# Routing edges to their nodes in two passes: chunks of 24 tiles, fixed rows for each digit, rows stored at their own fronts

## The chip, the core and the metric

The kernel runs on one core of a Trainium2 chip. The time is the device time of one launch in microseconds, the median of several runs; three runs of the kernel before took 8648.92, 8650.12 and 8655.76 us. A profile is one further execution with the hardware profiler on.

## What is computed

A message-passing layer on a graph of 10,000 nodes and 640,000 edges with random ends, 64 channels of 4 components:

```python
R = _silu(edge_feat @ w_rad)                              # (E, C)
xs = x[src]                                                 # (E, C, M)
tp = jnp.einsum('eci,ef,ifo->eco', xs, Y, cg)             # (E, C, M)
msg = R[:, :, None] * tp
agg = _segment_sum(msg.reshape(-1, C * M), dst, N).reshape(N, C, M)
return jnp.einsum('ncm,cd->ndm', agg, w_mix)
```

## The kernel before

The edges come in no order, and each must meet the sum of its node `dst`. So they are sorted by `dst` first, in two passes, as words of W = 9 floats: a key (14 bits of `src`, `dst` above them, a tag), the four of Y and the four of edge_feat. A tile is 128 edges, one a partition; there are 5000.

Pass 1 (`pass1`) sends each edge to one of 18 groups of 576 nodes in DRAM (`grp`), pass 2 (`pass2`) each word of a group to one of its 18 buckets of 32 nodes (`bkt`), 313 buckets in all. A bucket has room for BT = 17 tiles. All of it is done in three parts (`SPLIT`, 30, 35.5 and 34.5% of the edges), which take 5, 6 and 6 of the 17 tiles of a bucket: while one part is consumed, the next is sorted.

Both passes move words with the same two functions:

- `tables` counts, for the chunks of a batch, how many words of each digit (group or bucket) every tile has, and makes from the counts the place where each chunk's words of a digit begin (`sb`) and the row in DRAM where each of its 128 rows goes (`idx`). It is a chain of small operations on PE, ACT and DVE through one PSUM bank that all callers share.
- `route` takes chunk after chunk (12 tiles in pass 1, 11 in pass 2). `places`, `placed` and `slots` give each word a row and a slot within the row; rows have 14 or 15 slots and belong to one digit each. `spread` (line 519) multiplies a mask of slots (line 524) with the tile's words, so that each word stands in its slot of X and zeros elsewhere (line 527), and makes the one-hot of rows `oh`, six tiles on ACT (lines 542 and 543), the others on DVE (line 536). `move` multiplies the two on PE, tile by tile, into one PSUM bank (line 550); in pass 2 one more matmul (line 552) takes over the row that the chunk before left partly filled. `evict` copies to `rt` (line 557), and `store` writes 128 rows of 504 or 540 bytes with one indirect DMA from POOL (line 561). The stores of a pass are declared free of order among themselves.

A digit that has no room left sends rows to an overflow region.

`messages` then handles the buckets, in 939 units of 5 or 6 tiles. `gather` (line 817) fetches the 1024-byte rows of x by `src`, one indirect DMA a tile, five units ahead into seven buffers. `turn`, `turned`, `radial` and `silu` make R (lines 830 to 843), `spots` makes S, the one-hot of the node times Y (lines 851 and 854), `products` multiplies the gathered rows by R (line 861), and `sums` adds their outer products into G, 24 matmuls a unit (line 872). `evict` adds the sum of earlier parts, fetched by SP (lines 886 and 901), and `mix` applies the weights for four buckets.

Order: in the first stage part 0 goes through pass 1 alone, while the regions in DRAM are cleared. In `groups` the units of `messages` run in quarter steps, and steps of pass 2 for the next group and of pass 1 for the next part are put between them by the numbers that the generators yield (`HEAVY`) and that `pass2_steps` sums. PE, DVE and ACT issue in the order written there. The last group, which is smaller than the others (40 tiles, 9 buckets in part 0), comes first. At the end `overflow` (line 1031) takes what overflowed, 128 slots a round, through a loop that gathers, multiplies, reads the output rows, adds and writes them.

Of the kernel before, what the change touches and what calls it, by code (L numbers as in the profile page):

```python
# [18 lines left out]
F = mybir.dt.float32  # L19
# [6 lines left out]
P = 128  # L26
B = 18
W = 9
# [4 lines left out]
GN = B * NB  # L33
# [5 lines left out]
HEAVY = 4  # L39
BIG = 16384.0  # L40
FAR = 2097152.0


class Pass:


    def __init__(self, T, r, cap, act, carry):
        self.T, self.r, self.cap, self.act, self.carry = T, r, cap, act, carry
        self.stride = 1 << (cap + P - 1).bit_length()
        self.rw = r * W  # L50

        assert T * P + B * (2 * r - 2 if carry else r - 1) < (P + 1) * r and cap >= P
# [19 lines left out]
class Kernel:  # L72
    def __init__(self, ctx, tc, x, src, dst, Y, ef, w_rad, cg, w_mix, out):
# [8 lines left out]
        self.ef = ef.rearrange("(p t) f -> p t f", p=P)  # L82
        self.w_rad, self.cg, self.w_mix = w_rad, cg, w_mix
# [6 lines left out]
        N, E, T, r = self.N, self.E, 12, 14  # L90
        assert N <= 1 << 14 and BT == sum(sum(u) for _, u in SPLIT)
        self.NG = (N + GN - 1) // GN
        assert self.NG <= B
# [5 lines left out]
        self.gt = []  # L99
        for a, z in self.part:  # L100
            nch = (z - a + T - 1) // T
            e = [min(GN, N - g * GN) * (z - a) * P / N for g in range(self.NG)]
            self.gt.append([math.ceil((m + (r - 1) / 2 * nch + 4.5 * math.sqrt(m + (r * r - 1) / 12 * nch)) / P)
                            for m in e])
        NG = self.NG
        self.p1 = Pass(T, r, max(map(max, self.gt)) * P // r, 6, False)
        self.p2 = Pass(11, 15, BT * P // 15, 6, True)

        self.gbase = [[(k * NG + g) * self.p1.stride + self.p1.cap - self.gt[k][g] * P // r for g in range(NG)]
                      for k in range(len(SPLIT))]  # L110
        self.NBK = (N + NB - 1) // NB
# [5 lines left out]
        self.p1.ovf = len(SPLIT) * NG * self.p1.stride  # L117
        self.p2.ovf = self.NBK * self.p2.stride
        for q, tiles in ((self.p1, [z - a for a, z in self.part]), (self.p2, sum(self.gt, []))):
            q.none = -(-(q.ovf + sum((t + q.T - 1) // q.T for t in tiles) * P + 16) // q.stride) * q.stride  # L120
            q.rows = q.none
        self.p1.key, self.p2.key = "grp", "bkt"
        self.xw = max(q.T * q.rw for q in (self.p1, self.p2))
        assert max(q.T + q.carry for q in (self.p1, self.p2)) <= 12

        self.p1.NC, self.p2.NC = 24, max(-(-t // self.p2.T) for t in sum(self.gt, []))
        self.p1.dst = self.dr.tile([self.p1.rows, self.p1.rw], F, name="grp")
        self.p2.dst = self.dr.tile([self.p2.rows, self.p2.rw], F, name="bkt")

        self.sums = self.dr.tile([self.NBK, P, 256], F, name="sums")  # L130
        self.in_group = {"grp": 0, "bkt": 0}
# [10 lines left out]
    def consts(self):  # L142
# [8 lines left out]
        self.zr = c.tile([16, max(self.p1.rw, self.p2.rw)], F, name="zr")  # L151
# [8 lines left out]
        self.iB, self.i32 = self.dv[:, 0:B], self.dv[:, 0:NB]  # L160
# [8 lines left out]
        self.U2 = c.tile([32, 2, 32], F, name="U2")  # L169
        self.id2 = c.tile([64, 32], BF, name="id2")  # L170
        for h in range(2):
            nc.vector.tensor_copy(self.U2[:, h, :], self.U[:32, :32])
            nc.vector.tensor_copy(self.id2[32 * h:32 * h + 32, :], self.ident[:32, :32])
        for p in (self.p1, self.p2):

            p.on = c.tile([64, B * (p.T + 1)], F, name="on" + p.key)
            nc.vector.memset(p.on, 1.0)
            nc.vector.memset(p.on.rearrange("p (b t) -> p b t", b=B)[:, :, 0:1], 0.0)
            p.cols = c.tile([64, B * (p.T + 1)], F, name="cols" + p.key)
            nc.vector.memset(p.cols, 0.0)  # L180
        self.Ub = c.tile([P, P], BF, name="Ub")
        nc.vector.tensor_copy(self.Ub, self.U)
        self.A = c.tile([P, P], BF, name="A")
        nc.vector.scalar_tensor_tensor(self.A, self.ident, BIG, self.U, op0=OP.mult, op1=OP.add)
# [8 lines left out]

        self.gb, self.gc = [], []
        for k in range(len(SPLIT)):
            gb = iota("gb%d" % k, [[self.p1.stride, B]], base=k * self.NG * self.p1.stride)
            gc = c.tile([P, B], F, name="gc%d" % k)
            nc.vector.memset(gc, 0.0)
            for g in range(self.NG):
                nc.vector.memset(gb[:, g:g + 1], float(self.gbase[k][g]))  # L200
                nc.vector.memset(gc[:, g:g + 1], float(self.gt[k][g] * P // self.p1.r))
            self.gb.append(gb)
            self.gc.append(gc)

        self.k1 = c.tile([1, B], F, name="k1")
        self.k2 = c.tile([1, self.NG * B], F, name="k2")
# [3 lines left out]
        self.bb = iota("bb", [[self.p2.stride, B]])  # L210
        self.bn = iota("bn", [[NB, B]])
        self.bc = c.tile([P, B], F, name="bc")
        nc.vector.memset(self.bc, float(self.p2.cap))

    def clear_groups(self, k, eng):

        q = 2048
        for g in range(self.NG):
            n = self.gt[k][g] * W
            v = self.group_words(k, g)  # L220
            for o in range(0, n, q):
                m = min(q, n - o)
                eng.dma_start(v[:, o:o + m], self.z[:, :m])
                yield

    def group_words(self, k, g):

        o = self.gbase[k][g] * self.p1.rw
        v = self.p1.dst.rearrange("r w -> (r w)")[o:o + self.gt[k][g] * P * W]
        return v.rearrange("(p q) -> p q", p=P)  # L230

    def bucket_words(self, b, n, t0, t1):

        v = self.p2.dst[:self.p2.ovf, :].rearrange("(b s) w -> b (s w)", s=self.p2.stride)
        return v[b:b + n, t0 * P * W:t1 * P * W].rearrange("b (p q) -> p b q", p=P)

    def clear_buckets(self):
        nc, n = self.nc, 2048 // (BT * W)
        for b in range(0, self.NBK, n):
            m = min(n, self.NBK - b)  # L240
            nc.sync.dma_start(self.bucket_words(b, m, 0, BT),
                              self.z[:, :m * BT * W].rearrange("p (b q) -> p b q", b=m))
            yield
# [44 lines left out]
    def digits(self, D, dig, nt):  # L288

        for o in range(0, nt, 24):  # L290
            m = min(24, nt - o)
            self.onehot(D[:, o:o + m, :], dig[:, o:o + m], m)
            yield

    def onehot(self, D, dig, m):
        self.nc.vector.tensor_tensor(D, self.iB.unsqueeze(1).to_broadcast([P, m, B]),
                                     dig.unsqueeze(2).to_broadcast([P, m, B]), op=OP.is_equal)

    def floor(self, out, x, r, up, nm, n):

        nc = self.nc
        t = self.ph.tile([P, B], I32, name="ri", tag="ri" + nm, bufs=1)
# [3 lines left out]
    def tables(self, ps, D, nt, rows, kov, base, cap):  # L306
# [28 lines left out]
        if not ps.carry:  # L335
            self.floor(R[:H], n[:H], r, True, ps.key, H)
# [844 lines left out]
```

## Time and profile before

| | |
|---|---|
| median of the timed runs | 8650.12 us (8648.92 to 8655.76) |
| span of the profiled execution | 10572.8 us |
| mean granted clock of TensorE | 0.846 |
| indirect DMAs of POOL: gathers, stores | 5321, 958 |
| matmul instructions | 51381 |
| moved by DMA | 1057.31 MB, mean 100 GB/s |

The profiled execution is the slower one by 22%. Of its own time only the span is known. A float32 matmul is two instructions in the trace, each with a weight load (PEld) that can overlap it. In the groups of instructions, a row holds the line, engine, operation, out<-in with their shapes, the count, the busy time and the mean ns of one, and the idle time of the engine before them with what ended it.

### The profile page before, as it was taken

The page shows a single profiled execution, that of the slowest core. Times are in us where ns is not written, and L with a number is a line of the kernel's source. Part 1 is how long each engine was busy: PE and PEld are TensorE (multiplying, and loading weights), DVE is VectorE, ACT ScalarE, POOL GpSimd, SP SyncE. Part 2 cuts the span into 40 slices and gives each one's busy share as a digit, 9 for nine tenths or more (in the row PEclk, how much of TensorE's full clock was granted, in tenths as well). Part 3 has the DMA queues.
Part 4 walks back from the last instruction along what each step waited for, and adds up shares of the span by engine and source line. Part 5 has one row for each costly group of instructions (what it writes and reads, how often), then busy time and mean ns, then how long its engine had stood idle before and what let it go on. Part 6 is the DMA issues. An engine that isn't in the chain of part 4 may idle for free. (4 is left out here: it accounts for less than half of the span.)

```text
span 10572.8 us, 147096 instructions
## 1 busy us (share of the span) xinstructions
PE 8237.0 (78%) x51381; PEld 6957.0 (66%) x51381; DVE 6980.3 (66%) x12762; ACT 3997.5 (38%) x11789; POOL 6029.5 (57%) x6306
## 2 busy tenths in 40 slices
PE   6867877888788777787787787777777887878775
PEld 5756766667677666666676666656666666666664
DVE  6876767777776676776676776656565655656543
ACT  5754444444444343443343333322232222323220
POOL 1225655556565555566566655666666666666664
PEclk8978888888888888888888888878888888888887
DMA  8213333333333333333333333333333333333332
GB/s 165 78 40 90 96 93 90 94 95 97 94 98 92 95 92 103 105 108 111 102 105 110 109 104 104 103 110 112 104 99 104 104 100 106 100 106 99 104 106 74
DMA packets 696316, 1057.31 MB, mean 100 GB/s; under 512 B 251979, under 2 KB 500327, under 8 KB 695576
## 3 DMA queue, kind: packets, MB, share of 16 engines
q0 software_dynamic: 286560, 746.72, 24.8%
q1 hardware_dynamic: 406424, 293.41, 10.2%
q8 instruction: 406, 6.65, 0.3%
q10 hardware_dynamic: 2592, 7.78, 0.2%
q14 instruction: 334, 2.74, 0.1%
HBM read 856.49 MB, written 207.52 MB: 101 GB/s over the span
## 5 line engine op out<-in xcount | busy, mean ns | idle before, releaser
L817 POOL DMA_INDIRECT xg<-in_x_dram,sidx x5321 | 5057.6, 950 | 2989.6 <-issue 1374.4
L872 PE MATMUL G<-S,xg 128*128 128x128 f32 x21284 | 3223.2, 314 | 803.8 <-issue 408.1
L872 PEld LDWEIGHTS G<-S,xg 128*128 128x128 f32 x21284 | 3060.0, 228 | 924.5 <-issue 488.9
L550 PE MATMUL pr<-X,oh 128*128 128x126 f32 (+1 forms) x21286 | 3093.3, 302 | 696.8 <-issue 404.7
L550 PEld LDWEIGHTS pr<-X,oh 128*128 128x128 f32 x21286 | 2880.2, 212 | 928.4 <-issue 576.3
L861 DVE TENSOR_TENSOR xg<-xg,pre 128x1536 f32<-128x1536 f32 (+1 forms) x939 | 1557.4, 1659 | 587.0 <-ACT pre L843 440.0
L527 DVE TENSOR_TENSOR X<-dv,Wt 128x1485 f32<-128x1485 f32 (+5 forms) x958 | 1600.4, 1671 | 426.7 <-remote 182.3
L542 ACT ACTIVATE sq<-i,rowf 128x128 f32<-128x128 f32 x5658 | 1751.8, 394 | 9.9 <-DVE rowf L514 6.9
L843 ACT ACTIVATE pre<-pre 128x384 f32<-128x384 f32 (+1 forms) x939 | 429.1, 457 | 3098.6 <-remote 1406.6
L543 ACT ACTIVATE oh<-sq,ones 128x896 f32<-128x896 f32 (+2 forms) x958 | 937.3, 978 | 206.3 <-remote 57.9
L840 PE MATMUL pre<-wr,sT 54*128 54x384 f32 (+1 forms) x1878 | 902.0, 562 | 134.7 <-ACT sT L835 71.4
L854 DVE TENSOR_TENSOR S<-dv,pay 128x768 f32<-128x768 f32 (+1 forms) x939 | 857.3, 913 | 181.6 <-remote 86.2
L561 POOL DMA_INDIRECT bkt<-rt,idx x541 | 542.1, 1002 | 670.5 <-ACT rt L557 405.7
L561 POOL DMA_INDIRECT grp<-rt,idx x417 | 415.2, 996 | 791.7 <-ACT rt L557 388.2
L536 DVE TENSOR_TENSOR oh<-dv,rowf 128x640 f32<-128x640 f32 (+3 forms) x922 | 800.1, 868 | 0.4 <-remote 0.4
L901 DVE TENSOR_TENSOR Gs<-old,G 128x256 f32<-128x256 f32 x313 | 131.2, 419 | 1006.9 <-remote 552.4
L840 PEld LDWEIGHTS pre<-wr,sT 54*128 54x128 f32 (+1 forms) x1878 | 302.0, 200 | 386.5 <-issue 220.6
L901 DVE TENSOR_TENSOR Gp<-old,G 128x256 f32<-128x256 f32 x313 | 130.6, 417 | 538.1 <-remote 310.7
L557 ACT ACTIVATE rt<-pr 128x135 f32<-128x135 f32 (+1 forms) x958 | 257.3, 269 | 519.7 <-remote 230.9
L830 PEld LDWEIGHTS pre<-ident,pay 128*54 128x54 f32 (+1 forms) x939 | 109.0, 116 | 494.1 <-issue 310.3
L835 ACT ACTIVATE sT<-pre 54x128 f32<-54x128 f32 (+1 forms) x939 | 244.3, 260 | 429.5 <-remote 232.2
L830 PE MATMUL pre<-ident,pay 128*54 128x128 f32 (+1 forms) x939 | 294.1, 313 | 87.9 <-DVE xg L861 54.3
(214 smaller groups left out, 5296.4 us busy)
## 6 DMA issues: line engine op xcount, KB each, us to landing
xg<-in_x_dram,sidx POOLq DMA_INDIRECT x5321
sums<-Gp SPq DMA_DIRECT2D x626, 128.0 KB
old<-sums SPq DMA_DIRECT2D x626, 128.0 KB
bkt<-z SPq DMA_DIRECT2D x24, 994.5 KB
pay<-bkt SPq DMA_DIRECT2D x34, 486.0 KB
ys<-in_Y_dram SPq DMA_DIRECT2D x104, 96.0 KB
es<-in_edge_feat_dram SPq DMA_DIRECT2D x104, 96.0 KB
out_dram<-ot SPq DMA_DIRECT2D x69, 128.0 KB
```

The lines of the kernel that those rows point to most:

```text
L527: nc.vector.tensor_tensor(X[:, :m, :].rearrange("p t (s w) -> p t s w", w=W), msk.unsqueeze(3).to_broadcast([P, m, ps.r, W]), QD[c // Q][1 ...
L536: nc.vector.tensor_tensor(oh[:, :v, :], self.v128.unsqueeze(1).to_broadcast([P, v, P]), row[:, o:o + v].unsqueeze(2).to_broadcast([P, v, P ...
L542: nc.scalar.activation(sq[:, u, :], self.i128, AF.Square, bias=to, scale=-1.0)
L543: nc.scalar.activation(oh[:, v:v + len(at), :], sq[:, :len(at), :], AF.Relu, bias=self.ones[:, 0:1], scale=-2.0)
L550: nc.tensor.matmul(pr[:, :ps.rw], oh[:, u, :], X[:, u, :], start=(u == 0), stop=(not on and u == m - 1))
L561: st = nc.gpsimd.indirect_dma_start(out=ps.dst, out_offset=bass.IndirectOffsetOnAxis(ap=idx[:, i:i + 1], axis=0), in_=RT.pop(c), in_offset ...
L817: nc.gpsimd.indirect_dma_start(out=xg[:, t, :], out_offset=None, in_=self.x, in_offset=bass.IndirectOffsetOnAxis(ap=si[:, u:u + 1], axis=0))
L840: nc.tensor.matmul(R, ST_.pop(k)[:ut * W], self.wr[:ut * W, :ut * 64], start=True, stop=True)
L843: nc.scalar.activation(RT[k], RT[k], AF.Silu)
L854: nc.vector.tensor_tensor(S[:, :ut], self.eq[:, :ut].unsqueeze(3).to_broadcast([P, ut, NB, 4]), pb[:, :, 1:5].unsqueeze(2).to_broadcast([P ...
L861: nc.vector.tensor_tensor(V, V, R.unsqueeze(3).to_broadcast([P, ut, 64, 4]), op=OP.mult)
L872: nc.tensor.matmul(G[:, h].rearrange("p n f -> p (n f)"), V[:, t, 32 * h:32 * h + 32, :].rearrange("p c i -> p (c i)"), S[:, t].rearrange( ...
```

## The change

Both passes get another layout of a chunk. There are R rows for each digit, at fixed places: 6 for each of 20 groups in pass 1, 8 for each of 16 buckets in pass 2 (`Pass`: Q = B * R rows of 128). The words of a digit fill these rows by columns, so the n-th word of a digit stands in row n mod R, column n // R. A tile can only meet columns between bounds that are computed when the program is built: `lo[t]` (to which the count is raised if it is behind, leaving holes) and `hi[t]`, from the rates and a chance of 5e-9. `spread` makes X for those columns alone, in pieces of half a chunk and six tiles at a time, and `move` adds each tile into its own columns of PSUM.

```diff
-        N, E, T, r = self.N, self.E, 12, 14
+        N, E, T = self.N, self.E, 24
...
+        for t in range(T):
+            m = P * t * min(rates)
+            lo.append(max(0, int((m - low * math.sqrt(m)) // R)))
+            hi.append((surely(P * (t + 1), max(rates), miss) - 1) // R + 1)
...
+            for t, e, w in ps.spans(a, z):
+                m = e - t
+                msk = self.vmsk[:, :m * w].rearrange("p (t s) -> p t s", s=w)
...
+                nc.tensor.matmul(PR[c][:, ps.lo[t] * W:ps.hi[t] * W], oh[:, u, :], Xs[u],
+                                 start=(t == 0), stop=(t == sizes[c] - 1), skip_group_check=True)
```

A chunk is up to 24 tiles in both passes (the tiles of a group are split evenly) and is stored by one indirect DMA. Each of its Q rows is S columns long (39 in pass 1, 35 in pass 2) and goes to the row's own front in DRAM, where the chunk before ended; what it has of zeros behind its words is overwritten by the next chunk. So no row is carried over any more, and the stores are no longer declared free of order:

```diff
-            st = nc.gpsimd.indirect_dma_start(
-                out=ps.dst, out_offset=bass.IndirectOffsetOnAxis(ap=idx[:, i:i + 1], axis=0),
-                in_=RT.pop(c), in_offset=None, bounds_check=ps.none - 1, oob_is_err=False)
-            if self.in_group[ps.key]:
-                tc.declare_no_dep(st.ins, group=ps.key, reason="the rows of a pass are apart")
-            tc.add_to_no_dep_group(ps.key, st.ins)
-            self.in_group[ps.key] += 1
+            nc.gpsimd.indirect_dma_start(
+                out=ps.dst, out_offset=bass.IndirectOffsetOnAxis(ap=idx[:Q, i:i + 1], axis=0),
+                in_=RT.pop(c)[:Q, :], in_offset=None)
```

`tables` is rewritten for it and has 20-odd operations on DVE instead of some 45, and three trips through the shared PSUM bank instead of four to six. There are 20 groups of 15 or 16 buckets (the last one's buckets have 31 nodes) instead of 18 of 18; their words lie in 75 to 96 tiles a group and part. A group is loaded with 2 DMAs instead of 1, its buckets with 8 instead of 1:

```diff
+        for r in range(p.R):
+            self.nc.sync.dma_start(pay[r * s:(r + 1) * s, :nb, :],
+                                   rows[r][:, a:z].rearrange("b (p q) -> p b q", p=s))
```

If a chunk's words of a digit pass the end of the digit's room, all R rows of that digit go to an overflow block of R * S slots. `index` counts the words that arrive (`seen`), three more DVE operations a group; if the count is not E in the end, a new loop computes everything again edge by edge. `overflow` is called a third time for this.

In the schedule, each piece yields twice (`HALF` = 2) where a chunk yielded `HEAVY` = 4 once; `rt_bufs` goes from 38 to 16 in the first stage and from 5 to 3 in the second, the number of chunks in a batch of pass 1 (`NC`) from 24 to 12 and from 14 to 6.

More of the change, by code (lines that the diff above doesn't have):

```diff
@@ L226, in group_words @@
[L226 to L235, printed above, removed]
-    def clear_buckets(self):
[L238 to L243, printed above, removed]
+        self.bn = {n: iota("bn%d" % n, [[n, MB]]) for n in sorted({n for _, n, _ in self.grp})}
@@ new lines, in tables @@
+        nc.tensor.matmul(pre_p[:N, 0:B], self.ones[0:1, :N], rows, start=False, stop=True)
+        nc.tensor.matmul(pre_p[0:1, 64:64 + B], self.ones[:N, 0:1], n[:N], start=True, stop=True)
+        at = w("at", ps.T * B, 64)
+        sb = wk.tile([H, ps.T * B], BF, name="sb", tag="sb" + ps.key, bufs=3)
+        tb = lambda t: t[:, :m * B].rearrange("p (t b) -> p b t", b=B)
+        nc.vector.scalar_tensor_tensor(tb(at), sums[:, :, :m], float(B),
+                                       self.v128[:H, :B].unsqueeze(2).to_broadcast([H, B, m]), op0=OP.mult, op1=OP.add)
@@ L783, in quad @@
             (p, g), j, s = units[k]
-            n0 = (g * B + j - j % 4) * NB
-            return n0, min(n0 + 4 * NB, g * GN + GN, self.N) - n0
+            n0, b, nb = self.grp[g]
+            j -= j % 4
+            return [(n0 + i * b, min(b, self.N - n0 - i * b)) for i in range(j, min(j + 4, nb))]
         def tiles(k):
```

775 lines of the change are left out of this document (400 added, 375 removed).

## The prediction

> **What bounds the kernel now.** I read the head of the page first, then busy time by stage, then the timeline of POOL and PE in the main stage, then the groups of instructions that the change touches.
>
> ```profile
> span 10572.8 us, 147096 instructions
> PE 8237.0 (78%) x51381; PEld 6957.0 (66%) x51381; DVE 6980.3 (66%) x12762; ACT 3997.5 (38%) x11789; POOL 6029.5 (57%) x6306
> L817 POOL DMA_INDIRECT xg<-in_x_dram,sidx x5321 | 5057.6, 950 | 2989.6 <-issue 1374.4
> L561 POOL DMA_INDIRECT bkt<-rt,idx x541 | 542.1, 1002 | 670.5 <-ACT rt L557 405.7
> L561 POOL DMA_INDIRECT grp<-rt,idx x417 | 415.2, 996 | 791.7 <-ACT rt L557 388.2
> ```
>
> The profiled execution took 10572.8 us; the median of the timed runs is 8650.12. A fifth of the span is therefore not in an ordinary run, and no share of this page can be taken at its face. The stages (us, then busy time and count of PE, PEld, DVE, ACT, POOL, then granted clock):
>
> ```profile
> 0.00:617.00 617.00, 457.17 (x3381) 402.20 (x3381) 482.32 (x1058) 407.70 (x1223) 124.47 (x139) 0.90 0.48 108
> 617.00:842.00 225.00, 137.34 (x826) 116.84 (x827) 164.17 (x472) 107.11 (x313) 54.91 (x57) 0.71 0.16 42
> 842.00:10508.00 9666.00, 7626.65 (x47133) 6428.11 (x47132) 6311.57 (x11136) 3479.51 (x10241) 5839.12 (x6098) 0.85 0.36 101
> 10508.00:10573.00 65.00, 15.88 (x43) 9.81 (x43) 22.21 (x97) 3.20 (x13) 10.95 (x12) 0.54 0.05 13
> ```
>
> Part 0 is sorted alone until 617, the first groups are got ready until 842, then gathers, messages and the rest of the sorting run together, and the last 65 us are the overflow loops. In the main stage POOL issues 6098 indirect DMAs. How they follow each other, and what PE does beside them:
>
> ```profile
> 8721.97 0.95 POOL L817 DMA_INDIRECT xg<-in_x_dram,sidx  x1 [0.30 <-issue]
> 8723.22 0.95 POOL L817 DMA_INDIRECT xg<-in_x_dram,sidx  x1 [0.30 <-issue]
> 8724.47 1.01 POOL L561 DMA_INDIRECT bkt<-rt,idx  x1 [0.30 <-issue]
> 8701.30 0.37 PE L872 MATMUL G<-S,xg 128*128 128x128 f32 x1 [1.01 <-issue]
> 8702.70 1.06 PE L872 MATMUL G<-S,xg 128*128 128x128 f32 x3 [1.03 <-issue]
> 8710.47 2.84 PE L872 MATMUL G<-S,xg 128*128 128x128 f32 x24
> 5117.64 5.49 PE L872 MATMUL G<-S,xg 128*128 128x128 f32 x24 [0.65 <-DVE Gp L901]
> ```
>
> A gather takes 1.25 us from start to start, a store 1.30 to 1.32, with nothing to wait for. So the main stage needs POOL for 6098 x 1.26 = 7660 us. PE behaves otherwise: the same 24 matmuls take 2.84 us, or 5.49 after a pause (half clock), and at 8701 single ones stand a microsecond apart though they wait for nothing that is shown. I read these halts as part of what the profiled execution has over the timed ones. If the stages outside the main one are as long in a timed run, the main stage has 8650 - 842 - 65 = 7743 us there, of which POOL needs 7660, 99%. DVE has 6312 in it (82%). PE has 7627 at a granted clock of 0.85, and 0.85 of that, 6480, if it were at full clock all along. POOL is thus the bound that fits the median, with PE close behind if its clock stays low.
>
> **Stores, the gain.** The diff cuts part 0 into 62 chunks of 24 tiles, the others into 74 and 73, and each of 60 groups into 4: 449 stores for 958. In the first stage POOL is idle anyway, and 124 of the old and 62 of the new stores lie there. On the path go 834 - 387 = 447, at 1.30 us: -581 us. Rows grow from 504 or 540 B to 1404 or 1260 B, which the trace doesn't show; the nearest are a store of 128 rows of 1024 B, and one of 16 rows:
>
> ```profile
> L1112 POOL DMA_INDIRECT out_dram<-ocur,odi x3 | 3.1, 1028 | 25.0 <-DVE ocur L1111 25.0
> L1039 POOL DMA_INDIRECT bkt<-zr,zi x1 | 0.9, 877 | 3.5 <-DVEq L1044 3.5
> ```
>
> POOL pays mostly per instruction. I add 30 ns to each of 387 stores (+12); the bounds are 0 and +100.
>
> **The sorting work on DVE.** The columns a tile meets follow from the diff's bounds: 5 to 19 of them in pass 1, 4 to 16 in pass 2, 13.6 and 11.7 on average. That is not fewer words than before: 6 tiles at a time at the widest of them make 594, 756, 918 and 1026 elements in pass 1.
>
> ```profile
> L527 DVE TENSOR_TENSOR X<-dv,Wt 128x1512 f32<-128x1512 f32 x416 | 719.8, 1730 | 236.9 <-remote 117.1 <-PE pr L550 57.6 <-PE pre L830 24.7
> L527 DVE TENSOR_TENSOR X<-dv,Wt 128x675 f32<-128x675 f32 x17 | 14.6, 860 | 21.4 <-PE pp L489 6.3 <-PE pre L830 6.1 <-remote 5.8
> L527 DVE TENSOR_TENSOR X<-dv,Wt 128x270 f32<-128x270 f32 x17 | 7.5, 440 | 0.6
> L527 DVE TENSOR_TENSOR X<-dv,Wt 128x1485 f32<-128x1485 f32 (+5 forms) x958 | 1600.4, 1671 | 426.7 <-remote 182.3 <-PE pr L550 89.2 <-PE pre L830 42.0
> L524 DVE TENSOR_TENSOR dv<-dv,slot 128x165 f32<-128x165 f32 (+5 forms) x958 | 318.8, 333 | 11.8
> L524 DVE TENSOR_TENSOR dv<-dv,slot 128x75 f32<-128x75 f32 x17 | 4.0, 236 | 0.1
> L368 DVE TENSOR_TENSOR st<-inc,R 64x18 f32<-64x18 f32 x85 | 14.5, 170 | 2.7
> ```
>
> Three sizes give 0.16 us + 1.04 ns an element. The 1796 new products then sum to 1620 us, for 1600; the 1796 masks, some 80 elements at 0.24, to 445, for 319. The rows and slots are computed per 24 tiles instead of per 48 (some 670 more small operations at 0.19, of which a part is saved again: +90). Against that, a table falls from some 45 to some 21 operations, at 0.17 (L368), on 92 tables for 85: -320, of which 110 goes back to scans and casts twice as wide. Three more operations a group for the count of seen slots add 50. In all about +75 on DVE, half of it in the first stage: **DVE is not relieved**.
>
> A rule speaks for more: the Trainium skill (Perfetto Trace Analysis, Optimizing Scalar/DVE Operations) gives each DVE operation a fixed cost of about 60 ns on SBUF and 125 on PSUM. By it the 838 added pairs would cost an estimated 155 us; the rows' own intercepts, 0.16 us, are already in the sum and partly overlap with the next instruction, so the rule changes nothing there.
>
> **PE and ACT.** Pass 2 loses the 974 matmuls that carried a part row, and the squares for them; the tiles fall from 10643 to 10265.
>
> ```profile
> L552 PE MATMUL pr<-rt,oh 128*128 128x135 f32 x974 | 209.3, 293 | 52.6 <-issue 26.0 <-ACT rt L557 25.2 <-ACT Gp L903 0.4
> L550 PE MATMUL pr<-X,oh 128*128 128x135 f32 x11286 | 1646.8, 301 | 298.6 <-issue 178.3 <-ACT rt L557 101.2 <-DVE rk L456 6.2
> L550 PE MATMUL pr<-X,oh 128*128 128x126 f32 x10000 | 1450.4, 303 | 398.2 <-issue 226.4 <-ACT rt L557 78.7 <-DVE oh L536 61.6
> L542 ACT ACTIVATE sq<-i,tg 128x128 f32<-128x128 f32 x487 | 190.9, 392 | 0.0
> ```
>
> PE: -209, and 756 matmuls x 0.146 = -110. The width of a tile (45 to 171 columns) may matter or not: 126 and 135 columns cost the same 0.145 us. Below 126 I take no gain. By the Trainium skill (TensorE: Matmul & The Clock Gate, Step-by-step) a matmul streams one column a cycle; by that rule pass 1's ten tiles of over 128 columns would add an estimated 9% of 1450 us, 130. So PE loses 190 to 320 us of 7627, ACT some 350 of 3480, which frees nothing by itself.
>
> **Head.** Until 617 DVE sets the pace: it is busy 106.77 of the last 117 us of that stage.
>
> ```profile
> 500.00:617.00 117.00, 106.30 (x863) 97.33 (x861) 106.77 (x160) 99.35 (x293) 33.97 (x35) 0.99 0.09 27
> ```
>
> 24 tiles cost 4.06 us of products for 3.46, 1.04 of masks for 0.68, and 0.3 more for slots: +1.1 on 62 chunks, +68, less the tables' smaller part (-30): +40. The first group to be sorted in pass 2 had 40 tiles and 9 buckets and becomes 78 tiles and 16 buckets: the first gather starts later, but the 75 us in which POOL then stood without a second group go. I count 0 for it, between -20 and +80.
>
> **Tail.** A bucket over 2176 slots now sends its whole chunk to an overflow block of 8 rows x 35 slots, where before 15-slot rows overflowed. Placing the reference's own dst by the diff's rule (its seed is fixed) gives 6 such chunks and none in pass 1, and no key outside its columns: 6 x 280 = 1680 slots, 14 rounds of 128. Before there were three:
>
> ```profile
> 10519.51 0.15 DVE L1051 TENSOR_SCALAR osi<-opay 128x1 int32<-128x1 int32 x1 [2.83 <-DMA opay<-bkt]
> 10538.09 0.15 DVE L1051 TENSOR_SCALAR osi<-opay 128x1 int32<-128x1 int32 x1 [1.36 <-DMA opay<-bkt]
> 10555.54 0.15 DVE L1051 TENSOR_SCALAR osi<-opay 128x1 int32<-128x1 int32 x1 [1.42 <-DMA opay<-bkt]
> 10558.67 2.42 DMA ocur<-out_dram,odi
> ```
>
> A round is (10555.54 - 10519.51) / 2 = 18.0 us and nothing runs beside it: 11 x 18.0 = 198, and about 10 for the third, empty call and two operations more a round: +208.
>
> **What takes over.** The main stage shrinks from 7743 towards 7170, where DVE's 6340 are 88% and PE's 7300 at a clock of 0.85 would not fit at all; PE has to run warmer, as it does when it waits less. In-order engines that depend on each other don't all run at 88%. I give back a quarter of the gain, +150; the bounds are 0 and the whole 581. The loads of groups and buckets become 600 issues on SP for 108, each 0.3 to 0.4 us like its others; the eight of a group wait for one event, and SP, which holds the old sums and the partial sums behind them, has long waits of its own that cover 490 x 0.35 = 170 us (if not, that is what they cost):
>
> ```profile
> SPq L886 <- DVE dv L851: 1438.9, 175, 20.0
> SPq L905 <- ACT Gp L903: 1152.0, 137, 25.6
> ```
>
> Sum: 8650 - 581 + 12 + 40 + 208 + 150 = 8479, said as **8480**; its own range is 8340 to 8630.
>
> **Rivals.**
> 1. *PE's chain sets the pace* (slower). If the timed runs keep PE at a low clock, the main stage is PE's 7627, which also fits 7743, and POOL only follows it: its waits in the page are for G and for halts of PE. Then the stores bring nothing, PE's cut half of its 190 (it waits for DVE, which has more to do): 8650 - 95 + 40 + 208 = 8800. For it: POOL waits once a unit in the profile. Against it: PE's halts without a cause. It decides as soon as less than 260 of the 581 us arrive.
> 2. *All of the gain arrives*: DVE's 88% is no hindrance, 8330.
> 3. *Stores wait for stores.* New rows overlap the tails of their neighbours, and the exemption from ordering is gone, so each store waits on POOL's queue until the one before has landed, with gathers queued behind it. A small indirect DMA lands 2.42 us after its issue; 387 x 2.42 = 940 if each met its predecessor. The Trainium skill (DMA: Bandwidth & Descriptors, Two DMAs through the same engine are not ordered) says that only the completion semaphore orders them. But 387 stores in 7200 us stand 19 us apart and the wait is long over: 9400 has little for it.
> 4. *A key falls outside its columns*, and all 5000 tiles go through the loop, 90 ms: excluded by the count above.
>
> **How the numbers follow.** Forecast 0.44, rival 1 0.38, rival 2 0.10, rival 3 0.03, what I have not seen 0.05. The range goes from 8320, just under rival 2, to 8900, rival 1 with none of PE's cut and 100 us for DVE. A measurement of this kernel tells 0.2% (17 us). Faster: nearly all of the forecast and rival 2, 0.51; same 0.05, the border between forecast and rival 1; slower 0.44.
>
> **What would show it.** Right: 449 stores of about 1.03 us; in the main stage POOL's indirect DMAs 1.25 us apart over most of it; DVE's busy time near 7000 still; 14 rounds of 18 us in the tail; the first stage ending near 650. Wrong: POOL's idle time before gathers grows by what the stores left, and the main stage stays as long; or stores that idle on the landing of a store.

## The result, and the profile after

The changed kernel takes 8610.05 us (8608.17 to 8628.44) against 8650.12 for the kernel before: ratio 0.9955, 95% interval 0.9943 to 0.9968. A second measurement of the pair on another chip gave 8611.66 against 8635.02, 0.9973 [0.9961, 0.9986]. It is faster, clear of noise, by 0.3 to 0.45%; the forecast was 2%.

The profiled execution shown before, 10572.8 us, can't be compared with a profile of 8608 us. The kernel before was profiled once more, on a chip on which it takes 8628.69; that profile is "before" from here on. The head of its page, then that of the changed kernel:

```profile
span 8631.7 us, 147096 instructions
PE 7389.8 (86%) x51381; PEld 6373.0 (74%) x51381; DVE 6960.1 (81%) x12762; ACT 4020.4 (47%) x11789; POOL 6032.9 (70%) x6306
```

```profile
span 8608.1 us, 141721 instructions
PE 7366.7 (86%) x49106; PEld 6316.5 (73%) x49106; DVE 6967.2 (81%) x13381; ACT 3692.0 (43%) x10312; POOL 5578.9 (65%) x5982
```

POOL has 454 us less to do, ACT 328, and the span is 24 us shorter. Where the difference went is read from the first and the last gather. The rows of the gather line, before and after (count, min/median/max in ns, first and last start):

```profile
L817 POOL DMA_INDIRECT xg<-in_x_dram,sidx x5321: 940/946/1286, 672.2 to 8554.2; - x198
```

```profile
L808 POOL DMA_INDIRECT xg<-in_x_dram,sidx x5321: 940/946/1850, 738.2 to 8326.4; - x198
```

| us | before | after | difference | forecast |
|---|---|---|---|---|
| until the first gather | 672.2 | 738.2 | +66.0 | +40 |
| first to last gather | 7882.0 | 7588.2 | -293.8 | -419 |
| behind the last gather | 77.5 | 281.7 | +204.2 | +208 |
| span | 8631.7 | 8608.1 | -23.6 | -171 |

(-419 is -581 + 12 + 150.) Nearly all of the miss lies between the gathers. There the stages differ. Busy time by stage (us, PE, PEld, DVE, ACT, POOL, then granted clock, share of the DMA engines, GB/s), of before and after:

```profile
1000.00:5000.00 4000.00, 3526.23 (x25614) 3075.26 (x25614) 3564.35 (x6522) 2132.39 (x6298) 2974.80 (x3099) 0.93 0.43 125
5000.00:8000.00 3000.00, 2592.12 (x17350) 2209.20 (x17349) 2230.16 (x3862) 1122.52 (x3230) 2274.14 (x2379) 0.91 0.43 128
```

```profile
1000.00:5000.00 4000.00, 3575.55 (x24786) 3106.29 (x24784) 3587.54 (x6865) 2010.64 (x5648) 2750.05 (x2865) 0.92 0.46 129
5000.00:8000.00 3000.00, 2629.92 (x17112) 2238.98 (x17111) 2224.93 (x3877) 981.06 (x2722) 2263.26 (x2373) 0.90 0.49 137
```

At 1.26 us an indirect DMA, 3099 of them fill 98% of the first stretch before the change, and 2865 fill 90% after it. In the second stretch POOL is full in both (2379 and 2373, 100%). The sorting of later parts (pass 1) runs beside the messages until 5601 before and 5378 after (the last store to `grp`); PE and DVE are both busy for 88 to 90% of the first stretch in either kernel. In the second DVE is at 74%. Gathers alone in the same stretches, before and after, then stores alone, before and after:

```profile
1000.00:5000.00 4000.00, 2467.57 (x2594) 0.93 0.43 125
5000.00:8000.00 3000.00, 2016.10 (x2121) 0.91 0.43 128
```

```profile
1000.00:5000.00 4000.00, 2496.90 (x2615) 0.92 0.46 129
5000.00:8000.00 3000.00, 2152.96 (x2263) 0.90 0.49 137
```

```profile
1000.00:5000.00 4000.00, 507.23 (x505) 0.93 0.43 125
5000.00:8000.00 3000.00, 258.04 (x258) 0.91 0.43 128
```

```profile
1000.00:5000.00 4000.00, 253.15 (x250) 0.92 0.46 129
5000.00:8000.00 3000.00, 110.30 (x110) 0.90 0.49 137
```

From 5000 to 8000, 148 stores went (192 us at 1.30) and 142 more gathers took their place (178 us at 1.25): 92% of the time arrives. From 1000 to 5000, 255 stores went (332 us) and 21 more gathers came (26 us): 8%.

The ends make up the rest of the 294. At 1000 both kernels have issued 188 gathers, though the changed one began 66 us later: it has 26 stores fewer there (34 us), and POOL stands idle for about 30 us less. Behind 8000, 19 stores (25 us) went. So some 66 + 26 + 178 + 25 us arrive.

In 1000 to 5000 the time of the stores turned into a wait. POOL's longest wait in 1000 to 5000 that isn't its own issue, before and after (us in total, times, longest):

```profile
POOL xg L817 <- PE G L872: 86.2, 55, 10.7
```

```profile
POOL xg L808 <- PE G L863: 313.8, 114, 9.8
```

A gather waits here until the message sums of an earlier unit have read the buffer that it will fill. The loss isn't even within that stretch. Its first and its last quarter in the changed kernel:

```profile
1000.00:2000.00 1000.00, 887.39 (x6153) 774.91 (x6152) 885.18 (x1753) 545.10 (x1555) 659.64 (x686) 0.91 0.42 119
4000.00:5000.00 1000.00, 903.75 (x6299) 782.14 (x6297) 926.88 (x1701) 465.61 (x1278) 707.45 (x739) 0.92 0.50 140
```

POOL issues 86% of the time in the first and 93% in the last, while PE goes from 89 to 90% and DVE from 89 to 93%. POOL stands most where PE and DVE are less busy, so their busy share alone isn't what holds it.

The rest of the changed kernel's rows that answer to the prediction are these, groups of instructions first, then two of the 14 rounds of the tail in its timeline:

```profile
L499 DVE TENSOR_TENSOR X<-dv,Wt 128x918 f32<-128x918 f32 (+12 forms) x1796 | 1620.5, 902 | 163.8 <-PE pr L528 82.2
L496 DVE TENSOR_TENSOR dv<-dv,slot 128x102 f32<-128x102 f32 (+12 forms) x1796 | 445.9, 248 | 40.3
L546 POOL DMA_INDIRECT bkt<-rt,idx x240 | 239.5, 998 | 134.8 <-issue 57.2 <-ACT rt L539 31.6 <-ACT sT L826 15.3
L546 POOL DMA_INDIRECT grp<-rt,idx x209 | 213.0, 1019 | 678.4 <-ACT rt L537 477.7 <-DMA grp<-z 56.1 <-issue 43.1
L528 PE MATMUL pr<-X,oh 128*128 128x135 f32 (+14 forms) x20530 | 2754.9, 294 | 342.3 <-DVE oh L512 247.8 <-ACT rt L537 89.3 <-ACT oh L518 2.1
```

```profile
8374.13 0.15 DVE L1068 TENSOR_SCALAR osi<-opay 128x1 int32<-128x1 int32 x1 [1.40 <-DMA opay<-bkt]
8391.66 0.15 DVE L1068 TENSOR_SCALAR osi<-opay 128x1 int32<-128x1 int32 x1 [1.45 <-DMA opay<-bkt]
```

On two of the five chips used below PE halts between matmuls and every run, of the kernel before too, takes 19 to 24% longer; ratios of those batches are compared only with each other.

### The profile page after: what moved, and what is told of

Read it like the earlier page. It is cut to its first block, busy times and chain, and to the rows that moved or that the text cites. A ratio compares the mean times of both kernels' runs of the same rounds, so it can differ in the third digit from the quotient of the medians.

```text
span 8608.1 us, 141721 instructions
## 1 busy us (share of the span) xinstructions
PE 7366.7 (86%) x49106; PEld 6316.5 (73%) x49106; DVE 6967.2 (81%) x13381; ACT 3692.0 (43%) x10312; POOL 5578.9 (65%) x5982
## 5 line engine op out<-in xcount | busy, mean ns | idle before, releaser
L528 PE MATMUL pr<-X,oh 128*128 128x135 f32 (+14 forms) x20530 | 2754.9, 294 | 342.3 <-DVE oh L512 247.8
L528 PEld LDWEIGHTS pr<-X,oh 128*128 128x128 f32 x20530 | 2623.4, 202 | 507.9 <-DVE oh L512 281.7
L863 PE MATMUL G<-S,xg 128*128 128x128 f32 x21284 | 2933.0, 301 | 11.3 <-DVE Gs L892 5.2
L499 DVE TENSOR_TENSOR X<-dv,Wt 128x918 f32<-128x918 f32 (+12 forms) x1796 | 1620.5, 902 | 163.8 <-PE pr L528 82.2
L517 ACT ACTIVATE sq<-i,row 128x128 f32<-128x128 f32 x5388 | 1663.2, 390 | 47.8 <-DVE row L485 39.9
L518 ACT ACTIVATE oh<-sq,ones 128x768 f32<-128x768 f32 x898 | 838.4, 934 | 27.5 <-issue 1.7
L512 DVE TENSOR_TENSOR oh<-dv,row 128x768 f32<-128x768 f32 (+3 forms) x898 | 780.3, 873 | 0.2
L496 DVE TENSOR_TENSOR dv<-dv,slot 128x102 f32<-128x102 f32 (+12 forms) x1796 | 445.9, 248 | 40.3
L842 DVE TENSOR_TENSOR dv<-dv,dlc 128x192 f32<-128x192 f32 (+1 forms) x939 | 331.2, 353 | 18.1
L911 PE MATMUL po<-wf,Gs 128*128 128x256 f32 (+1 forms) x1280 | 306.8, 394 | 38.5 <-DVE over L420 31.5
```

The costliest lines, as they stand in the source:

```text
L496: nc.vector.tensor_tensor(msk, self.v128[:, :w].unsqueeze(1).to_broadcast([P, m, w]), slot[:, t:e].unsqueeze(2).to_broadcast([P, m, w]), o ...
L499: nc.vector.tensor_tensor(x, msk.unsqueeze(3).to_broadcast([P, m, w, W]), CH[c][1][:, t:e, :].unsqueeze(2).to_broadcast([P, m, w, W]), op= ...
L512: nc.vector.tensor_tensor(oh[:, :v, :], self.v128.unsqueeze(1).to_broadcast([P, v, P]), row[:, a:a + v].unsqueeze(2).to_broadcast([P, v, P ...
L517: nc.scalar.activation(sq[:, u - v, :], self.i128, AF.Square, bias=row[:, a + u:a + u + 1], scale=-1.0)
L518: nc.scalar.activation(oh[:, v:m, :], sq[:, :m - v, :], AF.Relu, bias=self.ones[:, 0:1], scale=-2.0)
L528: nc.tensor.matmul(PR[c][:, ps.lo[t] * W:ps.hi[t] * W], oh[:, u, :], Xs[u], start=(t == 0), stop=(t == sizes[c] - 1), skip_group_check=True)
```

## The experiments

The letters of theories mean what each expectation says. "Main" is the time from the first to the last gather, 7882 before and 7588 (7592 in the second profile) after the change.

**The kernel before as it is**, profiled once more.

> The kernel before, unchanged, for a second profile. Theory A (in the first profile PE was held up by something that the timed runs don't have): the span is near 8650 us, no single matmuls stand a microsecond apart, and POOL's indirect DMAs follow each other at 1.25 us over most of the main stage. Theory B (the halts belong to the kernel): the span is near 10570 again.

8633.75 us, profile 8631.7 us, PE with no pauses of about a microsecond between matmuls that wait for nothing. That is theory A. So the first profile's halts don't belong to the kernel on every chip, and with POOL at 98% in 1000 to 5000 and 100% in 5000 to 8000, POOL is the bound that fits an ordinary run.

**Half of the stores of before**, first try (the words of the left-out chunks are lost):

```diff
         def store(c):
+            if c % 2:
+                RT.pop(c)
+                return
```

> The kernel before without every second store of both passes (the words of those chunks are left out, so the overflow rounds go too, 54 us). All work of PE, DVE and ACT stays. Theory A (POOL bounds the main stage of the kernel before all along): some 410 stores at 1.30 us leave the path, 8650 - 530 - 54 = 8070. Theory B (DVE or PE sets the pace): 8650 - 54 = 8600. Theory C (DVE while both passes sort, POOL afterwards): only the stores after pass 1 is done count, some 170, 8650 - 220 - 54 = 8380.

8608.11, ratio 0.9977 [0.9967, 0.9987], the time of theory B: main is 7887.0, no shorter. But lost words have key 0, so their gathers all read row 0 of x, and this changes the gathers. Rows of this run, by stage and among POOL's waits:

```profile
1000.00:5000.00 4000.00, 3539.43 (x25669) 3088.07 (x25668) 3559.87 (x6512) 2137.62 (x6316) 2739.29 (x2869) 0.93 0.72 121
```

```profile
POOL xg L820 <- DMA xg<-in_x_dram,sidx: 85.2, 184, 3.8
```

The share of the DMA engines is 0.72 for 0.43 at fewer bytes, and gathers wait for gathers. The run says nothing on stores and was repeated with other indices (below).

**Eight of a chunk's one-hots on ACT for six**, in the kernel before, then in the changed one:

```diff
-        self.p1 = Pass(T, r, max(map(max, self.gt)) * P // r, 6, False)
-        self.p2 = Pass(11, 15, BT * P // 15, 6, True)
+        self.p1 = Pass(T, r, max(map(max, self.gt)) * P // r, 8, False)
+        self.p2 = Pass(11, 15, BT * P // 15, 8, True)
...
-            sq = self.ph.tile([P, 7, P], F, name="sq")
+            sq = self.ph.tile([P, 9, P], F, name="sq")
```

> The kernel before with eight one-hots of a chunk on ACT instead of six: DVE gets 2 x 0.133 us x 958 = 250 us less, ACT some 820 us more. Theory A (POOL bounds it): 8650 less only what the first stage gains (124 x 0.27 = 33), 8620. Theory B (DVE sets the pace): 8400. Theory C (DVE while both passes sort): 8480.

8623.18, ratio 0.9995 [0.9985, 1.0005], as theory A expected. DVE loses 104 us in 1000 to 5000 (3564 to 3461). Main gets 35 us shorter (7847.2), POOL going from 98 to 98.4% in that stretch, and the first gather comes 24 us later, so the time stays: before the change DVE holds POOL at most for the few per cent that it was idle.

The changed kernel, in the second stage alone:

```diff
-            sq = self.ph.tile([P, self.act, P], F, name="sq")
+            sq = self.ph.tile([P, self.act, P], F, name="sq", bufs=1)
...
-            self.rt_bufs, self.ls, self.act = 3, 4, 6
+            self.rt_bufs, self.ls, self.act = 3, 4, 8
```

> The changed kernel with eight one-hots of a piece on ACT instead of six in the second stage (and one buffer of squares for two): DVE 773 x 0.27 = 206 us less there, of which some 150 between 760 and 5000 us. Theory C (there DVE sets the pace, POOL only after 5000): 8610 - 150 = 8460. Theory D (PE, busy 89%, sets it): 8610. Theory A (POOL everywhere): 8610.

8685.05, ratio to before 1.0062 [1.0046, 1.0079], some 75 to 90 us slower than the changed kernel; none of the three theories has that. Its stage and two of PE's waits in it:

```profile
1000.00:5000.00 4000.00, 3565.49 (x24215) 3090.03 (x24215) 3388.67 (x6737) 2339.49 (x6486) 2685.60 (x2802) 0.90 0.44 126
```

```profile
PE pr L528 <- ACT rt L537: 127.7, 56, 5.9
PE pr L528 <- ACT oh L518: 42.8, 34, 3.7
```

DVE is 199 us less busy, ACT 329 more, and POOL issues 63 fewer DMAs: PE now waits 128 us for ACT's copies of `pr`, 72 in the changed kernel. ACT at 58% costs more than DVE's 5% bring. One buffer of `sq` for two was part of this edit, so how much of it is that buffer isn't told apart.

**Taking away clean.** Four runs on one chip: the changed kernel as it is, and three with one kind of work halved. In these three the gather indices come from a fixed table of spread rows, and words are left out or misplaced. No run has the table alone; the gathers' times (940/946 ns) stay as they were:

```diff
-            nc.vector.tensor_scalar(si[:, :m, :ut], key, (1 << 14) - 1, None, op0=OP.bitwise_and)
+            nc.vector.tensor_copy(si[:, :m, :ut], self.far[:, :m, :ut])
```

> The changed kernel as it is, beside the kernel before on the same chip, so that what is left out of it below has its own measure there. Where PE doesn't halt between matmuls: ratio to before 0.9955 as first measured, gathers waiting for G about 310 us between 1000 and 5000. On a chip where PE halts (before at about 10670): theory C says that PE is the bound all along and the stores bring what PE's smaller work brings, 190 to 320 us of 10670, ratio 0.97 to 0.985; theory P says 0.96 or less.

8611.66, ratio 0.9973 [0.9961, 0.9986]; 327 us of gathers waiting for G. As before.

Half of the stores of before again, with these indices:

> The kernel before without the store of every second chunk, spread gather indices, again beside the changed kernel. On a chip without halts: theory P 8050, theory C 8300 to 8400 with POOL idle before 5000 and full after it, theory N 8575. With halts: 0.954 of before, as on the chip of the batch before.

8305.83, ratio 0.9617 [0.9601, 0.9633]. Its gather line, and the gathers alone in the first stretch (2594 in before):

```profile
L823 POOL DMA_INDIRECT xg<-in_x_dram,sidx x5321: 940/946/1605, 658.2 to 8266.5; - x198
```

```profile
1000.00:5000.00 4000.00, 2535.24 (x2669) 0.93 0.43 125
```

Main is 7608.3, 274 shorter, for 386 stores fewer in it (502 us at 1.30): 55%, as theory C expected, with POOL at 93% in 1000 to 5000 and full behind it. The rest of the time saved is 41 us of the tail, where the left-out words take the overflow rounds with them, and a first gather 14 us earlier. So the old layout gives back about as large a part as the new one, 45% for 49%, and most of the loss comes with taking stores off POOL. Not all of it does: in 1000 to 5000 the stores fall from 505 to 274 (300 us) and 75 more gathers come (94 us), 31%, where the changed kernel has 8%. From 5000 to 8000 both get 92%. What the change put in place of the stores thus has a part in the first stretch, some 75 us by these shares; which of its steps it is wasn't tested. The wait for G has grown in the old layout too, from 86.2 us:

```profile
POOL xg L823 <- PE G L878: 233.8, 101, 14.2
```

Every second routing matmul of the changed kernel left out:

```diff
             for u in range(z - a):
                 t = a + u
+                if t % 2 and t != sizes[c] - 1:
+                    continue
```

> The changed kernel without every second routing matmul, spread gather indices, without the last overflow call, beside the changed kernel. On a chip without halts: if PE is one of the engines that hold the gathers back before 5000, 8160 to 8300 and less than 100 us of gathers waiting for G; if PE only follows, 8580 to 8610. With halts: 0.9175 of before as in the batch before, to be set against the changed kernel's own ratio there.

8231.99, ratio 0.9534 [0.9518, 0.955]. The gather line, the first stretch, and POOL's wait for G in it:

```profile
L813 POOL DMA_INDIRECT xg<-in_x_dram,sidx x5321: 940/946/1899, 737.9 to 8198.7; - x198
```

```profile
1000.00:5000.00 4000.00, 3277.26 (x20189) 2750.09 (x20189) 3696.74 (x7082) 2065.57 (x5802) 2835.62 (x2957) 0.85 0.46 133
```

```profile
POOL xg L813 <- PE G L868: 243.4, 96, 8.5
```

250 us of the difference are the tail: with so many words left out nothing overflows, which the expectation hadn't reckoned with, and the last call of `overflow` is left out too. So the time lies in the first of the expected ranges by the tail alone; with the tail added back, some 8480, it lies between the two. Main is 7460.8, 131 shorter. PE falls from 89 to 82% in the stage, DVE rises to 92%, POOL from 90 to 93%, and gathers still wait 243 us for G.

Half of DVE's one-hots in the changed kernel (the matmuls use a neighbour's):

```diff
+                v //= 2
                 nc.vector.tensor_tensor(oh[:, :v, :], self.v128.unsqueeze(1).to_broadcast([P, v, P]),
                                         row[:, a:a + v].unsqueeze(2).to_broadcast([P, v, P]), op=OP.is_equal)
```

> The changed kernel with half of VectorE's one-hot rows, spread gather indices, without the last overflow call, beside the changed kernel. On a chip without halts: VectorE alone holds the gathers 8380 to 8420, PE and VectorE hold each other 8480 to 8560, VectorE off the chain 8590 to 8610. With halts: 0.939 of before, as in the batch before.

8195.37, ratio 0.9493 [0.9477, 0.9509]. The same three views:

```profile
L813 POOL DMA_INDIRECT xg<-in_x_dram,sidx x5321: 940/946/1886, 686.0 to 8154.6; - x198
```

```profile
1000.00:5000.00 4000.00, 3652.40 (x25472) 3167.52 (x25471) 3508.21 (x7060) 2051.16 (x5770) 2830.92 (x2947) 0.92 0.47 133
```

```profile
POOL xg L813 <- PE G L868: 224.2, 100, 9.2
```

Again some 250 us of the difference are the tail, and 51 the head, where DVE sets the pace; without them, some 8495, the time is in the range where PE and VectorE hold each other. Main is 7468.6, 123 shorter. DVE falls to 88%, PE rises to 91%, POOL to 93%. Either engine's relief brings about the same small part and loads the other: neither alone holds the gathers. Both together weren't relieved.

The same three edits had run before, on a chip where PE halts, and the shares of the parts with them (below):

> The kernel before without the store of every second chunk (the words of those chunks are left out), and with gather indices taken from a fixed table of 1728 spread rows per partition, so that the gathers still read different rows. POOL has some 417 stores of 1.30 us less on the path: 542 us. Theory P (POOL is the only bound, every store off its queue is time): about 8050. Theory C (two in-order engines at 90% stand right behind POOL, and between 800 and 5000 us, where the sorting of later parts runs, they take over): about half of it arrives, 8300 to 8400, with POOL idle before 5000 and full after. Theory N (POOL isn't the bound): only the 54 us of the overflow rounds, 8575. The overflow rounds fall away in all three.

> The changed kernel without every second routing matmul of a chunk (its words are left out) and without the last overflow call; gather indices from a fixed table of spread rows. PE has about 1370 us less in all, some 1000 of them beside gathers. If PE is one of the engines that hold the gathers back before 5000 us, POOL gets full all along: 738 + 5708 x 1.255 + 260 = 8160, at most 8300. If PE only follows (theory P or DVE alone): 8580 to 8610. The waits of gathers for G in 1000 to 5000 (314 us in the changed kernel) go by the first, stay by the second.

> The changed kernel with half of the one-hot rows that VectorE makes for a chunk (the matmuls of the others use a neighbour's, so words land in wrong places) and without the last overflow call; gather indices from a fixed table of spread rows. VectorE has about 380 us less, ScalarE nothing more; some 280 us of them lie beside gathers, 200 before 5000. If VectorE alone holds the gathers there: 8380 to 8420. If PE and VectorE hold each other: 8480 to 8560. If VectorE isn't on the chain: 8590 to 8610.

Before took 10673.36 there, the three 10179.28, 9785.01 and 10030.43 (0.9539, 0.9175, 0.9388). None of the times expected holds; the parts of the last two that are tail aren't told apart there.

**Depth.** Fewer and more buffers for gathered rows in the changed kernel:

```diff
-LG = 5
+LG = 4
```

```diff
-LG = 5
+LG = 6
...
-            oh = self.ph.tile([P, ps.H, P], F, name="oh", bufs=3)
+            oh = self.ph.tile([P, ps.H, P], F, name="oh", bufs=2)
```

> The changed kernel with gathers 4 units ahead for 5, and 6 buffers of gathered rows for 7. Theory D (depth: the buffers are too few for uneven blocks): GpSimd loses more between 1000 and 5000 us, gathers wait for G 450 us or more for 327, time 8700 to 8800 for 8612. Theory T (throughput of PE and VectorE): 8600 to 8640.

> The changed kernel with gathers 6 units ahead and 8 buffers for 7; the room comes from two buffers of one-hots for three. Theory D: the waits for G fall below 250 us between 1000 and 5000, time 8520 to 8570 for 8612. Theory T: 8600 to 8620. If the third buffer of one-hots was needed: above 8620, and PE waits longer for one-hots than the 131 us it does.

Both ran on a chip where PE halts (before 10663.23): 10360.66 and 10377.07, 0.9713 [0.9697, 0.9729] and 0.9729 [0.9708, 0.975]. Their stages:

```profile
1000.00:5000.00 4000.00, 3250.59 (x20162) 2771.98 (x20161) 2909.36 (x5620) 1664.88 (x4705) 2215.17 (x2313) 0.83 0.36 103
```

```profile
1000.00:5000.00 4000.00, 3253.41 (x20160) 2773.32 (x20159) 2913.84 (x5620) 1663.26 (x4716) 2215.63 (x2314) 0.83 0.36 103
```

Six buffers or eight, POOL issues the same there; the run with eight has a buffer of one-hots less as well, and the two aren't told apart. The smaller one was run again where PE doesn't halt:

> The changed kernel with gathers 4 units ahead for 5 and 6 buffers for 7. Where PE doesn't halt: theory D (depth) 8700 to 8800 for 8612, gathers waiting for G 450 us or more for 327; theory T (throughput of PE and VectorE) 8600 to 8640 and waits for G as they were. Where PE halts: 0.971 of before, as measured.

8625.4 against 8626.9, ratio 0.9999 [0.999, 1.0009], main 7604.5, and gathers wait for G as long as before:

```profile
POOL xg L808 <- PE G L863: 323.6, 107, 11.5
```

Depth (theory D) falls on both kinds of chip: one buffer less costs 12 to 16 us of main, not 100. More than seven buffers were not tried where PE doesn't halt.

**Four one-hots on ACT for six** (`self.act` 4 in the second stage):

> The changed kernel with 4 one-hots of a piece on ScalarE for 6 while messages run; VectorE makes two more. If ScalarE's blocks in front of silu hold the chain: 8560 to 8590 for 8612, as 8 of them cost some 90. If VectorE's throughput holds it: its 200 us more cost about 90, 8680 to 8720, since 280 us less brought some 120.

10329.21 where PE halts, 0.9681 [0.9664, 0.9697], 0.3 and 0.5% under the two runs beside it, whose buffers differ. It wasn't run on another chip: where PE doesn't halt, what ACT's share is worth in this direction stays open.

**Other shares of the parts**, in the changed kernel:

```diff
-SPLIT = ((0.3, (5,)), (0.355, (6,)), (0.345, (6,)))
+SPLIT = ((0.317, (5,)), (0.355, (6,)), (0.328, (6,)))
```

> The changed kernel with shares 0.317, 0.355, 0.328 of the tiles for the three parts instead of 0.3, 0.355, 0.345. The reference's dst placed by the rule gives 3 overflow chunks for 6: 7 rounds of 18 us for 14, -126. The first part is 5% longer to sort: +35. If the main stage keeps its length: 8520. If less sorting beside gathers lets POOL run fuller before 5000 us: down to 8470. If the tail isn't counted as read (rounds hidden or cheaper): 8600 or more.

> The changed kernel with shares 0.317, 0.355, 0.328 again, on the chip of the runs beside it. Where PE doesn't halt: tail 126 us shorter by 7 rounds of 18, first gather 40 us later as in the run before (776.7 for 737), main stage some 30 us shorter since less sorting stands beside gathers: 8490 to 8530 for 8612.

> The changed kernel with shares 0.317, 0.355, 0.328. Where PE doesn't halt: tail 126 us shorter, first gather 38 later, main stage up to 30 shorter: 8490 to 8530 for 8612. Where PE halts: 0.958 of before, as measured.

Where PE halts: 10214.92 and 10220.36, 0.957 and 0.958 of before. Where it doesn't: 8511.35 (8505.84 to 8515.67), ratio 0.9866 [0.9849, 0.9882]. The gather line there:

```profile
L808 POOL DMA_INDIRECT xg<-in_x_dram,sidx x5321: 940/946/1825, 774.1 to 8349.3; - x198
```

First gather 36 later, main 7575.2 (13 shorter), and 157.7 us behind it (span 8507.0) for 281.7, seven rounds for 14, all as expected. It is 1.3% faster than the kernel before: the tail hid most of what the change brings.

## Why the prediction was right or wrong

- **POOL as the bound: right, for a part of the time.** In an undisturbed profile POOL issues 98% of the time between 1000 and 5000 and all of the time behind it, as was inferred from the median. DVE's relief by ACT brings 35 us of main in the kernel before, as much as POOL had idle time. PE's clock is 0.91, not the 0.85 that rival 1 leaned on, and PE is busy for 6844 of main's 7882 us.
- **Number and price of stores: right.** 6146 - 5699 = 447 DMAs less between first and last gather. Rows of 1404 B take 1.019 us, those of 1260 B 0.998, for 0.998 and 1.003: +22 ns at most, forecast +30.
- **DVE: right for the new products** (1620.5 and 445.9 us, forecast 1620 and 445), too high in all: 6960 to 6967, of which the rounds of the tail are 78 (24.7 to 102.3 behind the last gather), so -71 for +75. ACT loses 328, forecast 350.
- **PE: wrong.** The carried rows are gone, but PE loses 23 us in all, 80 without the tail's 57, for 190 to 320. The 20530 routing matmuls take 2754.9 us where before's 0.128 us each (2727.6 / 21286) would make 2631: 124 more. By the Trainium skill (TensorE: Matmul & The Clock Gate, Step-by-step), one column a cycle, they were estimated at 130 more. That the two are near is luck: over all tiles the columns fall from 131 to 112 on average, which by that rule makes the matmuls shorter. At 135 columns, which both kernels have, a matmul takes 288 ns for 286, but 156 ns of busy time for 130. Idle time ahead of these matmuls rose as well (192 to 342 us). So width isn't what costs the 124; what does stays open.
- **Head: +66 for +40.** DVE is busy for 661.8 us until the first gather, 565.8 before: +96, where +38 were reckoned; part of it lies beside other work. The three terms of a chunk, 0.60, 0.36 and 0.3, make 1.26 us and not 1.1, 78 us for 68. By 1000 us the delay of 66 is made up, by 34 us of stores and some 30 of POOL's pause before the second group, for which the prediction counted 0.
- **Tail: right**, +204 for +208, in 14 rounds of some 17.6.
- **"What takes over": the step that failed.** "I give back a quarter of the gain, +150" measured 287 (581 - 294), half of it. The mechanism stands: other engines take over where POOL leaves off, and halving the stores of the old layout shows it without the change's other parts (45% given back). The size was taken from means over the whole main stage, DVE at 88% and PE warmer. By stage, from the second profile, it can be read: the stores that go from 1000 to 5000 are worth 332 us, and 4000 - 332 = 3668 would need PE's 3576 and DVE's 3588 at 97 and 98%. In none of the undisturbed profiles does PE or DVE get past 92.4% of that stretch. Here both stay at 90%, and 8% of the 332 arrive: some 306 us are lost. From 5000 to 8000, with DVE at 74%, 92% arrive and some 14 us are lost. The 30 us of idle time that go at the start bring the sum down to the 287. The term was thus mis-sized by a stage in which nearly nothing arrives, which the means hid.
- **Rival 1's point of decision**, less than 260 of the 581, was missed by 34 us: 294 arrived. Its mechanism, PE alone at a low clock, isn't what took the rest: with PE at 82% POOL is still idle for 7% of the stage. **Rival 2** has its 92% from 5000 to 8000 only. **Rival 3** doesn't occur: of the stores to groups, 5 of 209 waited for another's landing, 15.4 us in all, and of the stores to buckets none is shown to. **Rival 4**, with its 90 ms, doesn't occur either.
- **The chances** gave 0.05 to a time that stays the same, between the forecast and rival 1. The measured 0.3 to 0.45% is closest to that.

What stays open: which of the many short waits between PE, DVE and ACT holds the last 10% of the stage, and which part of the change costs the stretch more than the stores alone do. Halving PE's routing matmuls or DVE's one-hots brings 131 and 123 us, one buffer less costs 12 to 16, and moving work to ACT loses; another order of the steps, or less work on PE and DVE together, was not tried.

## What to carry to other kernels

Where an engine is relieved, reckon the gain stage by stage: the time that leaves its queue is worth its full price only where the next engine has room, and less where two engines that feed each other are already at about 90%: here 8% of it arrived, and 31% in the old layout. Look for what the change adds outside the stage it relieves, such as a serial tail: here 204 us of 294 went there, and a shift of 1.7% of the work between parts got 124 of them back (for 36 in the head). When a profiled execution is far longer than the timed runs, get a second profile before sizing anything by its shares.

## What the runs showed of the hardware

- Chips differ in whether PE halts. In the batches of experiments the kernel before takes 8627 to 8635 us on three chips and 10663 to 10673 on two; none of the five was measured twice. Only the stage with gathers is longer there: with six buffers of gathered rows the changed kernel's first gather starts at 737.1 on a halting chip and at 737.2 on another, and main is 9332 for 7604. PE's timeline of the changed kernel with other shares, on a halting chip:

```profile
4317.19 0.36 PE L863 MATMUL G<-S,xg 128*128 128x128 f32 x1 [0.46 <-issue]
4319.29 0.39 PE L863 MATMUL G<-S,xg 128*128 128x128 f32 x2 [1.75 <-issue]
4321.42 0.37 PE L863 MATMUL G<-S,xg 128*128 128x128 f32 x1 [1.73 <-issue]
```

  Up to 1.75 us pass between matmuls of one unit with nothing to wait for. What causes it isn't known. Fewer stores bring more on such a chip: halving the stores of before takes 494 us off there (10673.36 to 10179.28) and 329 elsewhere, and the changed kernel with six buffers is at 0.9713 of before there and at 0.9999 elsewhere. The changed kernel as it is wasn't run on a halting chip, and why the gain is larger stays open.
- Gathers that mostly read one row are slow: with most indices at row 0 the DMA engines were busy for 0.72 of the stage against 0.43, at 121 for 125 GB/s, and main is 7887.0 where spread indices give 7608.3.
- A store of 120 rows of 1404 B costs POOL 2% more than one of 128 rows of 504 B (1.019 us for 0.998): here the bytes hardly count.
